# New figures in a list scheduler's tables, and the grouped attention's steps dealt out over all turns of the loop

## The chip, the cores and the metric

One core of a Trainium2 chip runs the kernel. The time is the device time of one execution in microseconds (us). Engines are named as in the profile: PE is TensorE, DVE VectorE, ACT ScalarE, POOL GpSimd and SP SyncE, which issues every load and store here. PEld is TensorE's weight load, SPq and PEq the sequencers.

## What is computed

Two attention blocks over cached keys and values, each with its own projections; their results stand side by side in the output. Block A has 32 query heads over 4 key heads (grouped), block B 32 over 32. All inputs are bf16.

```python
B, Sq, D = 16, 32, 1024;  Hq, Dh, Sk = 32, 128, 1024      # Hkv: 4 in A, 32 in B
q = (x @ wq).reshape(B, Sq, Hq, Dh).transpose(0, 2, 1, 3)
k, v = jnp.repeat(k_cache, Hq // Hkv, axis=1), jnp.repeat(v_cache, Hq // Hkv, axis=1)
p = softmax(einsum("bhqd,bhkd->bhqk", q, k) * Dh ** -0.5)
o = einsum("bhqk,bhkd->bhqd", p, v)
block = o.transpose(0, 2, 1, 3).reshape(B, Sq, Hq * Dh) @ wo
out = jnp.concatenate([block_A, block_B], axis=-1)
```

## The kernel before

`build` lists the work as operations, each with its engine, what it reads and writes, and a duration; `list_schedule` then puts them in the order in which each engine runs them. The 512 tokens are four groups G of 128.

**Block B** runs in 128 steps, one for each turn of the loop. A step (a quad) takes two batches by two heads. Its keys are one load of 1 MB into `KB_sb` (2 slots, L813), its values two loads of 0.5 MB into `VB_sb` (3 slots, L828). VectorE transposes the keys in 32x32 blocks into `KBt_sb` (two instructions, L848); a key slot is free when both are done. TensorE makes the scores as 32 matmuls on 32x32 tiles in `ps_s` (L887, entered as four operations of 8), ScalarE takes the exponential with the row sum (L907), TensorE transposes P (L921) into `ps_pt`, ScalarE copies that to `PT_sb`, TensorE multiplies with the values into `ps_o` (L971, 32 matmuls), VectorE normalizes into `OB_sb` (L987), and TensorE (L992, the OT transpose) and ScalarE turn the result into `OTB_sb`. Four quads share one `G` and one block of four heads.

**Block A** also has 128 steps, two for each key head and batch: `KA_sb` and `VA_sb` loads of 256 KB (L808, L820), key transposes on TensorE (L839) with a copy, scores (L865), exponential (L901), product with the values (L937, in `ps_kt`; GpSimd has copied them to `VAp_sb`, L822), normalizing (L947, L949) and a transpose (L955). A's steps are handed to the scheduler between B's: after turn t, as many as keep A at `t * NIT / NAS`, where `NIT` is 128 and `NAS = int(NIT * A_STEPS_FRAC)` is 117.

**Projections.** Queries come from `wq_sb` (four pieces of 256 KB each for A and B, L639), for A by heads (L657), for B by groups (L674); B's queries are also shuffled by TensorE into `QR` (L694). Output projections (L735) add into `acc` on VectorE (L748, L751 the last). All of these, the shuffles too, use one PSUM bank, `ps_pj`: each group must be copied out before the next may start. B's projections for the next block of heads are spread over the turns, and so are A's heads.

**What sets the order.** `list_schedule` keeps a clock for each engine and takes, of the operations that could start next within `look` microseconds of the earliest, the one with the longest remaining path. The durations of `DUR` (or the `dur=` at the operation), `lat` between engines, `DMA_BW` for a load's time, `DMA_MARGIN` (added to the time at which a load may be issued) and `MODE_SWITCH` (added on TensorE between kinds of tiles, `PE_MODE`) enter there, and nowhere in the program that results: engines then run in that order, each waiting on semaphores. SyncE too takes its loads strictly in the order that came out, and a load that waits for its buffer holds those behind it.

Before the loop stand the transposes of x, the first projections of B and the first heads of A.

Of the kernel before, what the change touches and what calls it, by code (L numbers as in the profile page):

```python
# [16 lines left out]
LAZY_PER_STEP = 100  # L17
LAZY_DELAY = 0
QSH_IN_PJ = True
A_STEPS_FRAC = 0.92  # L20
DMA_BW = 330.7e3
SP_STRICT = False
SP_AHEAD = 1.5
DMA_MARGIN = {"kb_dma": 0.5, "vb_dma": 0.5, "ka_dma": 0.5, "va_dma": 0.5}
DMA_MARGIN_DEFAULT = 2.0
PRIO_BONUS = {}
PE_MODE = {"scoresB": 2, "Qshuf": 2, "PVB": 1}
MODE_SWITCH = 0.11

DUR = {  # L30
    "scoresB": 1.1, "scoresA": 0.45, "PT_trB": 0.50, "PVB": 0.8, "OT_tr": 0.10, "KTA_tr": 0.50,
    "Qshuf": 0.25, "qprojA": 1.8, "qprojB": 1.8, "oprojA": 1.8, "oprojB": 0.9, "xT_tr": 0.5,
    "exp": 1.25, "expA": 1.05, "VAp_cp": 1.2, "normA@dve": 0.42, "OT_trA": 0.2, "OT_evA@dve": 0.35, "PT_ev@act": 0.52, "norm@act": 0.46, "OT_ev@act": 0.24, "KTA_ev@act": 0.93, "qA_ev@act": 0.52, "qB_ev@act": 0.52,
    "QR_ev@act": 0.31, "acc0": 0.52, "xT_ev@act": 0.93, "o_fin@act": 0.52,
    "KBt_tr": 1.15, "recip": 0.15, "norm@dve": 0.30, "PT_ev@dve": 0.62, "OT_ev@dve": 0.16, "KTA_ev@dve": 0.62,
    "QBt_tr": 0.35, "acc+": 0.62, "accF": 0.62, "qA_ev@dve": 0.62, "qB_ev@dve": 0.62, "xT_ev@dve": 0.62, "o_fin@dve": 0.62,
    "QR_ev@dve": 0.35,
    "c0": 0.2, "c1": 0.3,
}


# [20 lines left out]
class Prog:  # L62
# [102 lines left out]
                clk[("eng", op.eng)] = op.sig  # L165
            op.clock = clk

    def simulate(self, lat=0.12, dma_bw=DMA_BW, dma_lat=1.8, jitter=0.0, seed=0):
        rstate = [seed * 2654435761 % 2147483647 + 1]

        def uni(a_, b_):
            rstate[0] = (rstate[0] * 48271) % 2147483647
            return a_ + (b_ - a_) * (rstate[0] / 2147483647.0)
        free = {}
        dma_free = 0.0
        pe_mode = 0
        for op in self.ops:
            ready = 0.0
            for d in op.deps:
                if d.dma_key is None and d.eng == op.eng and op.eng == "pe":  # L180
                    continue
                if d.t1 + lat > ready:
                    ready = d.t1 + lat
            st = max(ready, free.get(op.eng, 0.0))
            jf = 1.0 + (uni(-jitter, jitter) if jitter else 0.0)
            if op.eng == "pe":
                m = PE_MODE.get(op.name, 0)
                if m != pe_mode:
# [12 lines left out]
        return max(op.t1 for op in self.ops)

    def list_schedule(self, lat=0.12, dma_bw=DMA_BW, dma_lat=1.8, look=0.35):
        ops = self.ops
        n = len(ops)
        users = [[] for _ in range(n)]
# [278 lines left out]
def build(nc, pa, pb, out):  # L485
# [13 lines left out]
    HS = 8  # L499
# [21 lines left out]
    with contextlib.ExitStack() as stack:  # L521
# [123 lines left out]
        def qprojA_head(s_, hh):  # L645
            h = s_ * HS + hh
            lazy_flush(("wq", 0, h // MS))
            hc = h % MS
            for t0 in range(0, NTOK, 512):
                tn = min(512, NTOK - t0)  # L650

                JS = 2 if DJ % 2 == 0 else 1
                for j0 in range(0, DJ, JS):
                    def e_qp(e, t0=t0, tn=tn, j0=j0):
                        last = None
                        for j in range(j0, j0 + JS):
                            last = e.matmul(ps_pj[:, 0:tn], wq_sb[:, 0, j, hc * Dh:(hc + 1) * Dh], xT_sb[:, 0, j, t0:t0 + tn],  # L657
                                            start=(j == 0), stop=(j == DJ - 1))
                        return last
                    pcs = sorted(set(j * WQP // DJ for j in range(j0, j0 + JS)))  # L660
                    pr.add("pe", e_qp, reads=[("wq", 0, k_) for k_ in pcs] + [("xT", 0, t) for t in range(NG)], writes=[BK_PJ], name="qprojA",
                           dur=0.225 * JS, rtag=dict((("wq", 0, k_), h // MS) for k_ in pcs))
                evac(QT_sb[:, s_ % 2, t0 // Sq:(t0 + tn) // Sq, hh, :], ps_pj[:, 0:tn].rearrange("p (b q) -> p b q", q=Sq),
                     reads=[BK_PJ], writes=[BK_PJ, ("QT", s_ % 2, hh)], name="qA_ev", wtag={("QT", s_ % 2, hh): s_})

        def qprojB(m_, G):
            lazy_flush(("wq", 1, m_))

# [53 lines left out]
        def oproj(pi, blk, G):  # L722
# [7 lines left out]
            for oh in range(NOH):  # L730
                for h0_ in range(0, nh, 2):
                    def e_op(e, oh=oh, h0_=h0_):
                        last = None
                        for hh in range(h0_, h0_ + 2):
                            last = e.matmul(ps_pj[:, 0:OUTW], OT[:, gp, hh, :], wo_[:, hh, oh * OUTW:(oh + 1) * OUTW],  # L735
                                            start=(hh == 0), stop=(hh == nh - 1))
                        return last
                    pr.add("pe", e_op, reads=[("OT", pi, gp, h0_), ("OT", pi, gp, h0_ + 1), (wo_res, h0_), (wo_res, h0_ + 1)], writes=[BK_PJ],
                           name="oprojA" if pi == 0 else "oprojB",
                           dur=0.45 * OUTW / 512, rtag={(wo_res, h0_): blk, (wo_res, h0_ + 1): blk, ("OTv", pi, gp): (blk, G)})  # L740
                a_ap = acc[:, pi, G, oh * OUTW:(oh + 1) * OUTW]
                o_ap = ost[:, oh * OUTW:(oh + 1) * OUTW]
                if nblk == 1:
# [109 lines left out]
        def st_scores(q):  # L853
# [3 lines left out]
            if q.pi == 0:  # L857
# [73 lines left out]
        def st_pvA(q):  # L931
# [32 lines left out]
        def st_pv(q):  # L964
# [228 lines left out]
```

## Time and profile before

| | |
|---|---|
| median of 3 runs (lowest, highest) | 917.7 us (912.47, 920.21) |
| profiled execution, its time | 913.31 us |
| its span in the trace | 911.5 us |
| mean granted clock of TensorE | 0.962 |
| busy: PE, DVE, ACT | 783.4, 519.3, 462.1 us |
| moved by SyncE's queue | 339.78 MB |

The span runs from the first to the last instruction. A view by windows gives each engine's busy time in a stretch, the number of its instructions, the granted clock as a share of full speed (PEclk), and the mean busy share and rate of the 16 DMA engines. Matmuls overlap, so what one costs is read from the starts of neighbouring groups.

### The profile page before, as it was taken

The page shows a single profiled execution, that of the slowest core. Times are in us where ns is not written, and L with a number is a line of the kernel's source. Part 1 is how long each engine was busy: PE and PEld are TensorE (multiplying, and loading weights), DVE is VectorE, ACT ScalarE, POOL GpSimd, SP SyncE. Part 2 cuts the span into 40 slices and gives each one's busy share as a digit, 9 for nine tenths or more (in the row PEclk, how much of TensorE's full clock was granted, in tenths as well). Part 3 has the DMA queues.
Part 4 walks back from the last instruction along what each step waited for, and adds up shares of the span by engine and source line. Part 5 has one row for each costly group of instructions (what it writes and reads, how often), then busy time and mean ns, then how long its engine had stood idle before and what let it go on. Part 6 is the DMA issues. An engine that isn't in the chain of part 4 may idle for free.

```text
span 911.5 us, 28186 instructions
## 1 busy us (share of the span) xinstructions
PE 783.4 (86%) x12610; PEld 432.9 (47%) x12610; DVE 519.3 (57%) x891; ACT 462.1 (51%) x853; POOL 67.9 (7%) x76
## 2 busy tenths in 40 slices
PE   5879999999998899988898789989897888978775
PEld 2325564545554454545454455536453445545332
DVE  1415655466645566555756556666665656666553
ACT  2215665655564455655564555555554544646242
POOL 0000000100110010101010010001010100001000
PEclk7879999999999999999999999999999899989898
DMA  9789899999999999999999999999999999899995
GB/s 333 270 302 370 308 399 361 402 385 390 359 380 409 411 349 400 401 381 392 368 405 403 411 374 390 375 346 397 405 408 399 385 398 403 333 409 397 385 410 190
DMA packets 151934, 341.64 MB, mean 375 GB/s; under 512 B 10496, under 2 KB 26880, under 8 KB 151808
## 3 DMA queue, kind: packets, MB, share of 16 engines
q1 hardware_dynamic: 151808, 339.78, 97.6%
q8 instruction: 101, 1.65, 0.7%
q14 instruction: 25, 0.20, 0.1%
HBM read 337.64 MB, written 2.10 MB: 373 GB/s over the span
## 4 chain that ended last, share of the span: by engine, by line
PE 56%; ACT 14%; DVE 13%; DMA 12%; issue 2%; SPq 2%; POOL 0%; POOLq 0%; DVEq 0%; ACTq 0%
PE ps_pj L735 10%; PE ps_s L887 10%; DVE KBt_sb L848 6%; PE ps_o L971 6%; PE ps_pj L657 6%; PE ps_pt L921 6%; ACT P_sb L907 5%; PE ps_pj L674 5%; PE ps_kt L937 4%; DMA KB_sb<-in_B_k_cache_dram 4%; ACT PTA_sb L901 3%; PE ps_s L865 3%; DMA wq_sb<-in_A_wq_dram 3%; DVE acc L748 3%; PE ps_kt L839 2%
## 5 line engine op out<-in xcount | busy, mean ns | idle before, releaser
L848 DVE STREAM_TRANSPOSE KBt_sb<-KB_sb 128x1024 f32<-128x1024 f32 x256 | 306.6, 1223 | 46.3 <-DMA KB_sb<-in_B_k_cache_dram 22.6
L887 PE MATMUL ps_s<-KBt_sb,QR 32*32 32x512 bf16 x4096 | 167.0, 402 | 13.8 <-ACT P_sb L907 7.4
L901 ACT ACTIVATE PTA_sb<-ps_s 128x1024 bf16<-128x1024 f32 x128 | 131.6, 1029 | 73.1 <-PE ps_s L865 59.9
L907 ACT ACTIVATE P_sb<-ps_s 128x1024 bf16<-128x1024 f32 x128 | 131.7, 1029 | 70.3 <-PE ps_pt L921 36.5
L588 ACT COPY PT_sb<-ps_pt 128x512 f32<-128x512 f32 x128 | 74.9, 585 | 150.6 <-PE ps_o L971 116.5
L822 POOL COPY VAp_sb<-VA_sb 128x1024 bf16<-128x1024 bf16 x64 | 66.6, 1040 | 770.5 <-DMA VA_sb<-in_A_v_cache_dram 667.3
L921 PE MATMUL ps_pt<-id,P_sb 128*128 128x128 f32 x512 | 91.7, 302 | 18.4 <-ACT P_sb L907 16.9
L987 DVE TENSOR_SCALAR OB_sb<-ps_o,rinv_all 128x128 bf16<-128x128 f32 x128 | 44.4, 347 | 108.0 <-PE ps_o L971 107.6
L921 PEld LDWEIGHTS ps_pt<-id,P_sb 128*128 128x128 f32 x512 | 74.2, 208 | 43.2 <-ACT P_sb L907 25.2
L971 PE MATMUL ps_o<-VB_sb,PT_sb 128*32 128x128 bf16 x4096 | 84.9, 224 | 8.4 <-DMA VB_sb<-in_B_v_cache_dram 6.7
L865 PE MATMUL ps_s<-QT_sb,KTA_sb 128*128 128x256 bf16 x512 | 85.3, 275 | 4.2 <-ACT PTA_sb L901 2.2
L735 PE MATMUL ps_pj<-woB_sb,OTB_sb 128*128 128x512 bf16 x256 | 75.4, 391 | 12.9 <-DVE acc L748 5.4
L937 PE MATMUL ps_kt<-VAp_sb,PTA_sb 128*128 128x129 bf16 x1024 | 80.3, 221 | 5.4 <-ACT KTA_sb L588 2.3
L971 PEld LDWEIGHTS ps_o<-VB_sb,PT_sb 128*32 128x32 bf16 x4096 | 60.1, 98 | 52.1 <-issue 38.7
L657 PE MATMUL ps_pj<-xT_sb,wq_sb 128*128 128x512 bf16 x256 | 74.0, 406 | 11.4 <-DMA wq_sb<-in_A_wq_dram 4.2
L887 PEld LDWEIGHTS ps_s<-KBt_sb,QR 32*32 32x32 bf16 x4096 | 49.7, 90 | 67.5 <-issue 19.5
L937 PEld LDWEIGHTS ps_kt<-VAp_sb,PTA_sb 128*128 128x128 bf16 x1024 | 64.9, 98 | 31.2 <-issue 13.4
L674 PE MATMUL ps_pj<-wq_sb,xT_sb 128*128 128x512 bf16 x256 | 71.0, 391 | 4.3 <-ACT QR L588 1.8
L735 PE MATMUL ps_pj<-woA_sb,OTA_sb 128*128 128x512 bf16 x256 | 66.9, 389 | 7.4 <-DVE ost L751 4.7
L588 ACT CAST QR<-ps_pj 128x256 bf16<-128x256 f32 x128 | 48.5, 379 | 46.0 <-PE ps_pj L694 43.3
L748 DVE TENSOR_TENSOR acc<-acc,ps_pj 128x512 f32<-128x512 f32 x64 | 43.5, 680 | 44.6 <-PE ps_pj L735 44.2
L865 PEld LDWEIGHTS ps_s<-QT_sb,KTA_sb 128*128 128x128 bf16 x512 | 44.3, 98 | 32.3 <-ACT PTA_sb L901 5.8
(52 smaller groups left out, 574.0 us busy)
## 6 DMA issues: line engine op xcount, KB each, us to landing
KB_sb<-in_B_k_cache_dram SPq DMA_DIRECT2D x128, 1024.0 KB, 8.2
VB_sb<-in_B_v_cache_dram SPq DMA_DIRECT2D x256, 512.0 KB, 8.9
KA_sb<-in_A_k_cache_dram SPq DMA_DIRECT2D x64, 256.0 KB, 9.5
VA_sb<-in_A_v_cache_dram SPq DMA_DIRECT2D x64, 256.0 KB, 7.7
wq_sb<-in_B_wq_dram SPq DMA_DIRECT2D x32, 256.0 KB, 6.9
wq_sb<-in_A_wq_dram SPq DMA_DIRECT2D x32, 256.0 KB, 8.7
woB_sb<-in_B_wo_dram SPq DMA_DIRECT2D x32, 256.0 KB, 8.4
woA_sb<-in_A_wo_dram SPq DMA_DIRECT2D x32, 256.0 KB, 7.8
```

The source lines that it names most:

```text
L588: pr.add("act", lambda e: e.copy(dst_ap, src_ap), reads=reads, writes=writes, name=name + "@act", wtag=wtag, rtag=rtag)
L657: last = e.matmul(ps_pj[:, 0:tn], wq_sb[:, 0, j, hc * Dh:(hc + 1) * Dh], xT_sb[:, 0, j, t0:t0 + tn], start=(j == 0), stop=(j == DJ - 1))
L674: last = e.matmul(ps_pj[:, 0:CW], xT_sb[:, 1, j, G * P:(G + 1) * P], wq_sb[:, 1, j, :], start=(j == 0), stop=(j == DJ - 1))
L735: last = e.matmul(ps_pj[:, 0:OUTW], OT[:, gp, hh, :], wo_[:, hh, oh * OUTW:(oh + 1) * OUTW], start=(hh == 0), stop=(hh == nh - 1))
L848: pr.add("dve", lambda e: e.transpose(KBt_sb[:, sl, t_, :].bitcast(F32), KB_sb[:, rs, t_, :].bitcast(F32)), reads=[("KB", rs)], writes=[(" ...
L865: last = e.matmul(ps_s[:, sbf, c2, i * 2 * P:(i + 1) * 2 * P], KTA_sb[:, sl, c * P:(c + 1) * P], qt, start=True, stop=True)
L887: last = e.matmul(ps_s[32 * cg:32 * cg + 32, sbf, g2, :].rearrange("p (s j) -> p s j", s=16), lhsT, rhs, start=(fp == 0), stop=(fp == 3), ...
L901: pr.add("act", lambda e: e.activation(dst, src, ACTF.Exp, scale=scale), writes=BK_S[sbf] + [("PTA", q.half)], name="expA", rtag={("Sv", s ...
L907: pr.add("act", lambda e: e.activation(dst, src, ACTF.Exp, scale=scale, accum_out=stat[:, 0:1]), writes=BK_S[sbf] + ["P", "rowsum"], name= ...
L921: last = e.transpose(ps_pt32[:, m * P:(m + 1) * P], p32[:, m:Sk // 2:NPK], id32[:])
L937: last = e.matmul(ps_kt[:, qh * OA0:qh * OA0 + Dh + 1], PTA_sb[:, h, c, qh * P:(qh + 1) * P], VAp_sb[:, sl, 4 * h + c, 0:Dh + 1], start=(h ...
L971: last = e.matmul(ps_o[32 * a:32 * a + 32, 0:Dh], PT_pairs[:, c // 2, 32 * a:32 * a + 32, c % 2], VB_sb[:, kvs, a // 2, a % 2, c, :], star ...
```

## The change

New figures in the scheduler's tables: durations of operations, the latency between engines, the DMA rate and margins, and `look`. `A_STEPS_FRAC` becomes 1.0, so `NAS` is 128 and A's steps are dealt out evenly over all turns. No operation is added or removed; two lines fewer stand in the file, so that L887 is L885 afterwards, L971 is L969, and so on.

```diff
-A_STEPS_FRAC = 0.92
-DMA_BW = 330.7e3
+A_STEPS_FRAC = 1.0
+DMA_BW = 390e3
...
-DMA_MARGIN = {"kb_dma": 0.5, "vb_dma": 0.5, "ka_dma": 0.5, "va_dma": 0.5}
-DMA_MARGIN_DEFAULT = 2.0
+DMA_MARGIN = {}
+DMA_MARGIN_DEFAULT = 1.0
...
 DUR = {
-    "scoresB": 1.1, "scoresA": 0.45, "PT_trB": 0.50, "PVB": 0.8, "OT_tr": 0.10, "KTA_tr": 0.50,
...
+    "scoresB": 0.222, "scoresA": 0.222, "PT_trB": 0.235, "PVA": 0.312, "PVB": 0.116, "OT_tr": 0.08, "OT_trA": 0.16,
...
-    def list_schedule(self, lat=0.12, dma_bw=DMA_BW, dma_lat=1.8, look=0.35):
+    def list_schedule(self, lat=0.2, dma_bw=DMA_BW, dma_lat=1.8, look=0.1):
...
-                           writes=BK_S[sbf], name="scoresB", dur=0.275, tag="B%d" % q.t,
+                           writes=BK_S[sbf], name="scoresB", dur=0.222, tag="B%d" % q.t,
...
-                       dur=0.2, tag="B%d" % q.t, rtag={"PT": q.qid, ("VB", kvs, 0): q.kid, ("VB", kvs, 1): q.kid}, wtag={"Ops": q.qid})
+                       dur=0.116, tag="B%d" % q.t, rtag={"PT": q.qid, ("VB", kvs, 0): q.kid, ("VB", kvs, 1): q.kid}, wtag={"Ops": q.qid})
```

What it moves, at three places. The first is SyncE's queue near the start, from the second pieces of wq on. Before:

```order
L639 DMA wq_sb<-in_B_wq_dram 128x2x512 x3
L639 DMA wq_sb<-in_A_wq_dram 128x2x512 x4
L639 DMA wq_sb<-in_B_wq_dram 128x2x512
L828 DMA VB_sb<-in_B_v_cache_dram 128x2x1024 x2
L808 DMA KA_sb<-in_A_k_cache_dram 128x1024
L820 DMA VA_sb<-in_A_v_cache_dram 128x1024
L813 DMA KB_sb<-in_B_k_cache_dram 128x2x2048
L718 DMA woB_sb<-in_B_wo_dram 128x1024 x4
L708 DMA woA_sb<-in_A_wo_dram 128x1024
L639 DMA wq_sb<-in_A_wq_dram 128x2x512 x4
L708 DMA woA_sb<-in_A_wo_dram 128x1024 x5
L813 DMA KB_sb<-in_B_k_cache_dram 128x2x2048
```

Now, from B's output weights on, which stood behind those pieces:

```order
L716 DMA woB_sb<-in_B_wo_dram 128x1024 x4
L811 DMA KB_sb<-in_B_k_cache_dram 128x2x2048
L637 DMA wq_sb<-in_B_wq_dram 128x2x512 x4
L637 DMA wq_sb<-in_A_wq_dram 128x2x512 x4
L806 DMA KA_sb<-in_A_k_cache_dram 128x1024
L818 DMA VA_sb<-in_A_v_cache_dram 128x1024
L811 DMA KB_sb<-in_B_k_cache_dram 128x2x2048 x2
L826 DMA VB_sb<-in_B_v_cache_dram 128x2x1024 x4
L811 DMA KB_sb<-in_B_k_cache_dram 128x2x2048
L637 DMA wq_sb<-in_A_wq_dram 128x2x512 x4
L706 DMA woA_sb<-in_A_wo_dram 128x1024 x8
```

The fifth key load of B stands ahead of all second wq pieces, and four key loads stand ahead of the third wq pieces of A (the last x4 row), where one stood.

The second is TensorE at the same time, about where A's first heads run (`ps_pj<-xT_sb,wq_sb` is a head's projection, x8 for one head). Before:

```order
L992 MATMUL ps_o<-ident,OB_sb 128x128
L657 MATMUL ps_pj<-xT_sb,wq_sb 128x512 x32
L865 MATMUL ps_s<-QT_sb,KTA_sb 128x256 x4
L694 MATMUL ps_pj<-QBt,ident 32x256 x4
L865 MATMUL ps_s<-QT_sb,KTA_sb 128x256 x4
L674 MATMUL ps_pj<-wq_sb,xT_sb 128x512 x2
L887 MATMUL ps_s<-KBt_sb,QR 32x512 x32
```

Now, some rows earlier in the program:

```order
L885 MATMUL ps_s<-KBt_sb,QR 32x512 x32
L655 MATMUL ps_pj<-xT_sb,wq_sb 128x512 x8
L919 MATMUL ps_pt<-id32,P_sb 128x128 x4
L969 MATMUL ps_o<-VB_sb,PT_sb 32x128 x32
L672 MATMUL ps_pj<-wq_sb,xT_sb 128x512 x8
L990 MATMUL ps_o<-ident,OB_sb 128x128
L885 MATMUL ps_s<-KBt_sb,QR 32x512 x32
L969 MATMUL ps_o<-VB_sb,PT_sb 32x128 x32
L655 MATMUL ps_pj<-xT_sb,wq_sb 128x512 x8
```

B's second quad was scored behind A's heads 4 to 7 and A's first steps; now all four quads of B's first group stand between the heads.

The third is TensorE in the loop, around the 45th quad of B (in the trace of before these rows run from 353 to 359 us). Before:

```order
L887 MATMUL ps_s<-KBt_sb,QR 32x512 x24
L694 MATMUL ps_pj<-QBt,ident 32x256 x4
L887 MATMUL ps_s<-KBt_sb,QR 32x512 x8
L921 MATMUL ps_pt<-id32,P_sb 128x128 x4
L992 MATMUL ps_o<-ident,OB_sb 128x128
L735 MATMUL ps_pj<-woB_sb,OTB_sb 128x512 x2
L865 MATMUL ps_s<-QT_sb,KTA_sb 128x256 x4
L735 MATMUL ps_pj<-woB_sb,OTB_sb 128x512 x2
L887 MATMUL ps_s<-KBt_sb,QR 32x512 x16
L971 MATMUL ps_o<-VB_sb,PT_sb 32x128 x32
```

Now, at the 46th quad:

```order
L885 MATMUL ps_s<-KBt_sb,QR 32x512 x32
L655 MATMUL ps_pj<-xT_sb,wq_sb 128x512 x8
L953 MATMUL ps_kt<-ident,OA_sb 128x128 x2
L990 MATMUL ps_o<-ident,OB_sb 128x128
L919 MATMUL ps_pt<-id32,P_sb 128x128 x4
L863 MATMUL ps_s<-QT_sb,KTA_sb 128x256 x4
L969 MATMUL ps_o<-VB_sb,PT_sb 32x128 x32
L733 MATMUL ps_pj<-woA_sb,OTA_sb 128x512 x8
L990 MATMUL ps_o<-ident,OB_sb 128x128
```

A quad's scores stand in one row of 32 where they were cut by shuffles and projections. Over the whole fast program the scores of B take 153 rows (220 before), the products with B's values 128 (141) and the shuffles 121 (125).

## Rows read from the trace of the kernel before

**Rows 1.** The page's busy times, shares and instruction counts of each engine.
```profile
PE 783.4 (86%) x12610; PEld 432.9 (47%) x12610; DVE 519.3 (57%) x891; ACT 462.1 (51%) x853; POOL 67.9 (7%) x76
```

**Rows 2.** Windows over the span: engines, PEclk, DMA share, GB/s.
```profile
core 0: us, PE busy (x) PEld busy (x) DVE busy (x) ACT busy (x) POOL busy (x), PEclk, DMA share, GB/s
0.00:75.00 75.00, 53.77 (x425) 24.32 (x425) 21.69 (x30) 20.47 (x32) 4.37 (x14) 0.82 0.85 303
75.00:100.00 25.00, 23.55 (x391) 13.32 (x378) 13.19 (x26) 14.31 (x27) 2.08 (x2) 1.00 0.87 324
100.00:850.00 750.00, 666.62 (x11067) 375.99 (x11052) 455.25 (x782) 405.63 (x744) 61.38 (x59) 0.98 1.01 388
850.00:911.50 61.50, 39.43 (x758) 19.28 (x758) 29.15 (x54) 21.73 (x51) 0.10 (x1) 0.88 0.84 324
```

**Rows 3.** Windows: the two best stretches of 25 us.
```profile
300.00:325.00 25.00, 21.92 (x376) 12.19 (x364) 14.53 (x24) 11.79 (x24) 2.08 (x2) 0.93 1.04 410
800.00:825.00 25.00, 20.82 (x365) 11.87 (x366) 14.62 (x25) 12.24 (x26) 2.08 (x2) 0.86 1.04 411
```

**Rows 4.** Windows: two of four milder stretches; first, last and sum of the six lowest.
```profile
250.00:275.00 25.00, 23.04 (x368) 14.03 (x350) 12.81 (x25) 15.48 (x27) 3.12 (x3) 1.00 1.01 377
375.00:400.00 25.00, 22.53 (x327) 12.43 (x324) 17.95 (x27) 13.40 (x24) 2.08 (x2) 1.00 1.02 385
...
225.00:250.00 25.00, 23.76 (x399) 13.67 (x391) 15.83 (x31) 13.46 (x24) 3.12 (x3) 1.00 0.96 361
...
775.00:800.00 25.00, 22.17 (x388) 12.87 (x388) 16.64 (x30) 16.05 (x31) 2.08 (x2) 1.00 0.91 339
sum 150.00, PE 136.98 PEld 77.49 DVE 101.14 ACT 78.80 POOL 14.56; mean PE 22.83 PEld 12.92 DVE 16.86 ACT 13.13 POOL 2.43
```

**Rows 5.** Timeline of TensorE: start, duration, engine, line, operation; two groups with their successors.
```profile
99.14 1.13 PE L887 MATMUL ps_s<-KBt_sb,QR 32*32 32x512 bf16 x32
100.20 0.75 PE L921 MATMUL ps_pt<-id,P_sb 128*128 128x128 f32 x4
...
342.83 0.43 PE L887 MATMUL ps_s<-KBt_sb,QR 32*32 32x512 bf16 x8
343.19 0.28 PE L955 MATMUL ps_kt<-ident,OA_sb 128*128 128x128 bf16 x2
```

**Rows 6.** Waits: engine, line, awaited: us in total, times, longest.
```profile
PEld ps_pt L921 <- ACT P_sb L907: 25.2, 27, 1.8
PEld ps_o L992 <- DVE OB_sb L987: 21.3, 51, 1.0
PEld ps_pj L694 <- ACT QR L588: 20.1, 29, 1.6
PEld ps_pj L735 <- DVE acc L748: 15.0, 24, 1.3
...
DVE KBt_sb L848 <- DMA KB_sb<-in_B_k_cache_dram: 22.6, 22, 2.3
```

**Rows 7.** Timeline of SyncE at the start, and one row of its waits.
```profile
40.57 2.59 SPq L639 DMA_DIRECT2D wq_sb<-in_B_wq_dram  x3
...
49.01 0.68 SPq L813 DMA_DIRECT2D KB_sb<-in_B_k_cache_dram  x1
...
61.37 1.92 SPq L639 DMA_DIRECT2D wq_sb<-in_A_wq_dram  x4
...
69.64 0.38 SPq L813 DMA_DIRECT2D KB_sb<-in_B_k_cache_dram  x1
...
SPq L639 <- PE ps_pj L657: 10.9, 5, 9.1
```

**Rows 8.** Groups by line: busy us, mean ns, idle before; A's largest and smallest matmul group, B's largest.
```profile
L848 DVE STREAM_TRANSPOSE KBt_sb<-KB_sb 128x1024 f32<-128x1024 f32 x256 | 306.6, 1223 | 46.3 <-DMA KB_sb<-in_B_k_cache_dram 22.6 <-PE ps_s L887 18.9 <-PE ps_o L971 2.4
L887 PE MATMUL ps_s<-KBt_sb,QR 32*32 32x512 bf16 x4096 | 167.0, 402 | 13.8 <-ACT P_sb L907 7.4 <-DVE KBt_sb L848 4.4 <-ACT QR L588 1.2
L865 PE MATMUL ps_s<-QT_sb,KTA_sb 128*128 128x256 bf16 x512 | 85.3, 275 | 4.2 <-ACT PTA_sb L901 2.2 <-ACT QT_sb L588 0.7 <-DVE KTA_sb L590 0.3
L955 PE MATMUL ps_kt<-ident,OA_sb 128*128 128x128 bf16 x128 | 17.8, 221 | 1.3 <-DVE OA_sb L949 1.0
```

More of the change, by code (lines that the diff above doesn't have):

```diff
@@ L30 @@
 DUR = {
-    "scoresB": 1.1, "scoresA": 0.45, "PT_trB": 0.50, "PVB": 0.8, "OT_tr": 0.10, "KTA_tr": 0.50,
[L32 to L38, printed above, removed]
+    "scoresB": 0.222, "scoresA": 0.222, "PT_trB": 0.235, "PVA": 0.312, "PVB": 0.116, "OT_tr": 0.08, "OT_trA": 0.16,
+    "KTA_tr": 0.62, "Qshuf": 0.11, "qprojA": 0.434, "qprojB": 0.434, "oprojA": 0.434, "oprojB": 0.434, "xT_tr": 0.62, "exp": 1.23,
+    "expA": 1.03, "PT_ev@act": 0.587, "OT_ev@act": 0.27, "OT_evA@dve": 0.3, "QR_ev@act": 0.38, "KTA_ev@act": 1.01,
+    "KTA_ev@dve": 0.685, "qA_ev@act": 0.59, "qA_ev@dve": 0.69, "qB_ev@act": 0.59, "qB_ev@dve": 0.69, "acc0": 0.59, "acc+": 0.68,
+    "accF": 0.68, "xT_ev@act": 1.01, "xT_ev@dve": 0.69, "KBt_tr": 1.23, "QBt_tr": 0.435, "recip": 0.15, "norm@dve": 0.347,
+    "normA@dve": 0.4, "VAp_cp": 1.04, "c0": 0.2, "c1": 0.3,
 }
@@ L166, in finalize, with simulate @@
             op.clock = clk
-    def simulate(self, lat=0.12, dma_bw=DMA_BW, dma_lat=1.8, jitter=0.0, seed=0):
+    def simulate(self, lat=0.2, dma_bw=DMA_BW, dma_lat=1.8, jitter=0.0, seed=0):
         rstate = [seed * 2654435761 % 2147483647 + 1]
@@ L661, in qprojA_head @@
                     pr.add("pe", e_qp, reads=[("wq", 0, k_) for k_ in pcs] + [("xT", 0, t) for t in range(NG)], writes=[BK_PJ], name="qprojA",
-                           dur=0.225 * JS, rtag=dict((("wq", 0, k_), h // MS) for k_ in pcs))
+                           dur=0.217 * JS, rtag=dict((("wq", 0, k_), h // MS) for k_ in pcs))
                 evac(QT_sb[:, s_ % 2, t0 // Sq:(t0 + tn) // Sq, hh, :], ps_pj[:, 0:tn].rearrange("p (b q) -> p b q", q=Sq),
@@ L676, in qprojB @@
                 pcs = sorted(set(j * WQP // DJ for j in range(j0, j0 + JS)))
-                pr.add("pe", e_qp, reads=[("wq", 1, k_) for k_ in pcs] + [("xT", 1, G)], writes=[BK_PJ], name="qprojB", dur=0.225 * JS,
+                pr.add("pe", e_qp, reads=[("wq", 1, k_) for k_ in pcs] + [("xT", 1, G)], writes=[BK_PJ], name="qprojB", dur=0.217 * JS,
                        rtag=dict((("wq", 1, k_), m_) for k_ in pcs))
@@ L739, in oproj @@
                            name="oprojA" if pi == 0 else "oprojB",
-                           dur=0.45 * OUTW / 512, rtag={(wo_res, h0_): blk, (wo_res, h0_ + 1): blk, ("OTv", pi, gp): (blk, G)})
+                           dur=0.434 * OUTW / 512, rtag={(wo_res, h0_): blk, (wo_res, h0_ + 1): blk, ("OTv", pi, gp): (blk, G)})
                 a_ap = acc[:, pi, G, oh * OUTW:(oh + 1) * OUTW]
@@ L866, in e_st @@
                         return last
-                    pr.add("pe", e_st, reads=[("QT", q.s % 2, a) for a in range(HS)] + [("KTA", sl)], writes=BK_S[sbf], name="scoresA", dur=0.225,
+                    pr.add("pe", e_st, reads=[("QT", q.s % 2, a) for a in range(HS)] + [("KTA", sl)], writes=BK_S[sbf], name="scoresA", dur=0.222,
                            tag="A%d" % q.t, rtag=dict([(("QT", q.s % 2, a), q.s) for a in range(HS)] + [(("KTA", sl), q.kid)]),
@@ L940, in st_pvA @@
             for c0 in (0, 2):
-                pr.add("pe", lambda e, c0=c0: e_pv(e, c0), reads=[("PTA", h), ("VAp", sl)], writes=[BK_KT], name="PVA", dur=0.32, tag="A%d" % q.t,
+                pr.add("pe", lambda e, c0=c0: e_pv(e, c0), reads=[("PTA", h), ("VAp", sl)], writes=[BK_KT], name="PVA", dur=0.312, tag="A%d" % q.t,
                        rtag={("PTA", h): q.qid, ("VAp", sl): q.kid}, wtag={"OpsA": q.kid})
```

## The prediction

> **What bounds the kernel now.** I read the busy shares first [rows 1]. TensorE, VectorE and ScalarE are all partly idle, TensorE least: it is busy 783.4 us, 86% of the span. Beside it stand the transfers. All 339.78 MB of them are issued by SyncE, and the next view shows when they flow. In the four long stretches [rows 2] the core moved 303 GB/s up to 75 us, 324 up to 100 us, 388 from 100 to 850 us and 324 at the end. The best single stretches reached 410 and 411 GB/s, and TensorE was no fuller there than elsewhere [rows 3]. So about 405 GB/s is what transfers do here when nothing holds them. At 405 the 339.78 MB would take 839 us. The span is 72 us longer; that is where any gain has to come from.
>
> Where is it lost? From 0 to 100 us the kernel moved 0.303 x 75 + 0.324 x 25 = 30.8 MB, which at 405 takes 76 us: 24 us lost. Between 100 and 850 us the loss is (1 - 388/405) x 750 = 31 us, most of it in a few stretches: six of 25 us, one about every 100 us, fell to 339 GB/s at the lowest and 354 in the mean [rows 4]. At 405 those 150 us would be 131: 19 us. In them TensorE is busy 22.83 of 25 us, against 20.82 and 21.92 in the best stretches. The last stretch loses (1 - 324/405) x 61.5 = 12 us. The remaining 5 are the 1.9 MB that the queues moved besides, and rounding.
>
> So the kernel alternates. Where projections crowd TensorE, buffers come free late and transfers thin out; elsewhere transfers are the limit. Two kinds of TensorE time in the crowded stretches can be removed by order alone: breaks and short waits.
>
> **What a break costs.** A B quad's scores are 32 matmuls on 32x32 tiles. In one piece they take 100.20 - 99.14 = 1.06 us to the next group; a piece of 8 takes 343.19 - 342.83 = 0.36 us [rows 5]. That is 0.029 us a matmul, so 8 are worth 0.23, and 0.13 us is paid for each piece, on leaving it. Entering may cost as much again, which these rows don't settle: 0.13 to 0.26 a piece.
>
> **What the waits cost.** TensorE's weight loads stood idle 21.3 us for OB (51 times), 20.1 us for QR and 15.0 us for acc, the last two because every projection and shuffle shares the one bank ps_pj. For the exponential ahead of the P transposes it stood 25.2 us, 27 times [rows 6].
>
> **The change, part by part.**
>
> *The start.* Before, SyncE's queue put the second wq pieces, each waiting for a projection on TensorE, ahead of the fifth B key load. The wq rows issue at 40.57 and 61.37 us, and the key loads behind them at 49.01 and 69.64 us [rows 7]; SyncE waited up to 9.1 us on one such wq buffer. In the new order the first of these key loads is ahead of the wq pieces and three more stand before the wq_A pieces that wait for heads 4 to 7, while TensorE scores all four quads of the first B group among the first heads. I take 350 GB/s for the first 75 us, half the way from 303 to 405: 22.7 MB in 65 us, 10 us saved, and half the deficit of 75 to 100 us, 3 us. Against that, heads 4 to 7 now find their wq_A behind the woB and key loads, which is 2 MB or some 5 us of transfers, with only the tail of a B quad on TensorE to cover it; I charge 3 us. Net **-10** (0 to -24).
>
> *Fewer breaks.* In the order the scores stand in 153 rows instead of 220, PV of B in 128 instead of 141, the shuffles in 121 instead of 125: 84 pieces fewer. At 0.13 to 0.26 us that is 11 to 21 us of TensorE, say 16.
>
> *Fewer and other waits.* I laid the durations of the trace rows over the rows that stand between producer and consumer. Of 128 OT transposes, 60 had under 0.5 us of other TensorE work behind their PV; now 28. Of 287 groups in ps_pj, 105 were followed by the next user too soon for the evacuation; now 52. The other way: 14 P transposes stood within 1.3 us of their scores, now 34. Halving 21.3 and 20.1 + 15.0 us gives 28 us; 20 more short exponentials at 25.2 / 27 = 0.93 us take back 19. Net 9 us, between -28 and +19.
>
> Together 25 us of TensorE over 911 us, 2.7%. It counts only where TensorE is the limit. That is the six stretches, four milder ones at 377 to 385 GB/s [rows 4], and half the rest of the loop at most: 250 us fully and 500 us at a third make 417 us; 2.7% of it is 11. I take **-10** (bounds: all breaks and halved waits everywhere -34; the new exponential waits alone +12).
>
> *A spread out.* NAS goes from 117 to 128, so A's 128 steps no longer stand in the first 117 turns at 1.094 a turn. A's six matmul groups sum to 365.0 us of matmul time, B's and x's eight to 570.5 [rows 8], so A is 39% of TensorE's work, and 8.6% less of it per turn is 3.4% of TensorE in turns 0 to 116. In the ten stretches, 250 us, that is **-8** (0 to -12). At the end it comes back: 11 turns' worth, 8.6% x 39% x 783 = 26 us of TensorE goes into the last stretch, where it was busy 39.4 of 61.5 us [rows 2]. The free 22 us hold most of it: **+3** (0 to +10). Transfers lose nothing in bytes.
>
> *DMA at 390 instead of 330.7, margins 1.0, smaller look.* No instruction changes; all of it acts through the order counted above. The lowest stretch shows 339 [rows 4] and the best 411 [rows 3], so 390 sits beside the loop's own 388. The Trainium skill, "DMA: Bandwidth & Descriptors", section Specifications, lists an HBM limit of about 358 GB/s per core; by it the old 330.7 was the better figure and no reordering could help a kernel that already averages more. The trace doesn't agree: 388 over 750 us [rows 2].
>
> Sum: -10 - 10 - 8 + 3 = -25. The profiled execution took 913.3 us (span 911.5), so 888 on its own scale. It lies under the median of the runs, 917.7, by a factor 1.0048: **892 us**.
>
> **The rivals.**
>
> *A. Only the start gains.* If 388 GB/s is what this mix of loads can do, because wq rows of 1 KB and wo rows are slower than keys, TensorE's relief in the loop is idle time moved elsewhere. For it: transfers count as busy throughout (share 1.01 from 100 to 850 us). Against: rates below 370 only where TensorE is fullest. 913 - 10 + 3 = 906, on the median 910. Chance 0.17; about half of it beyond 1%. By the page's 358 GB/s the result would be this one or no change; the 411 in rows 3 is why I give it no more.
>
> *B. Slower: VectorE held by late keys.* VectorE runs in order, and KBt transposes now stand where a 390 GB/s queue would have delivered. In the weight-heavy stretches the queue gives 354: over six of 25 us it falls (1 - 354/390) x 150 = 14 us behind, and over the first 100 us, at 308, another 21. What stands behind a waiting transpose on VectorE are norm, acc and KTA copies, and TensorE waits for these. Now VectorE waits 22.6 us for keys, 22 times, 1 us each [rows 6]. If the 35 us come on top and the start gains nothing, 913 - 18 + 3 + 35 = 933, median 937. It decides from the point where these waits pass about 50 us in all. Against: the same lag also means later buffers for nobody, and VectorE is busy 519.3 us in all, 306.6 of it with these transposes [rows 1, 8], so there is room to catch up. Chance 0.11.
>
> *C. The loop saturates.* If relief and even spreading let transfers reach 405 almost everywhere, 24 us at the start less 5, and 25 of the loop's 31 go: 913 - 44 = 869, median 873. Chance 0.12.
>
> **How the numbers follow.** Forecast (880 to 904) 0.60, A 0.17, B 0.11, C 0.12. A run within 1% of 917.7 (908.5 to 926.9) counts as no change, about what a measurement of this kernel can tell. Faster: 0.60 + 0.12 + some 0.06 of A = 0.78; the rest of A and a little of B is same, 0.12; slower 0.10. The range must reach C's 873 with a margin and A's 910 with one: 868 to 915, leaving out B and the outer edges.
>
> **What would show it.** Right: the first 75 us above 340 GB/s and no SyncE wait near 9 us at a wq load; the lowest 25 us stretch of the loop above 355; TensorE's idle for OB near 11 us, that for the exponential up by ten or more; TensorE fuller than 39 of the last 61 us. Wrong: VectorE waiting over 50 us for KB_sb (B), loop rate still 388 with TensorE less busy (A), or TensorE saturated and transfers thin after 850 us, which would mean that spreading A cost more than 10 us at the end.

## The result and the profile after

The changed kernel takes 874.8 us (median of 4 runs, 873.4 to 881.4) where the kernel before took 918.7 in the same comparison: a ratio of 0.955, 95% interval 0.948 to 0.961. Ratios here and below are of the means of the fast executions, so they can differ a little from the ratio of two medians. The profiled execution took 873.43 us with a span of 871.6, 39.9 us less than the span before. The prediction was 892 us in a range of 868 to 915; the sign and the range held, and the gain was 1.6 times the 25 us forecast on the span's scale.

The same four stretches of the changed kernel, in windows over the span (engines' busy time with instruction counts, PEclk, DMA share, GB/s; the last one is shorter because the span is):

```profile
0.00:75.00 75.00, 56.32 (x611) 29.85 (x620) 29.40 (x42) 27.44 (x47) 4.32 (x14) 0.98 1.00 376
75.00:100.00 25.00, 24.43 (x373) 16.21 (x380) 12.06 (x25) 15.83 (x27) 4.16 (x4) 1.00 0.91 336
100.00:850.00 750.00, 641.12 (x11324) 389.80 (x11434) 461.70 (x805) 414.56 (x772) 59.30 (x57) 0.98 1.04 403
850.00:871.60 21.60, 10.94 (x195) 5.61 (x182) 8.16 (x21) 4.75 (x11) 0.10 (x1) 0.92 0.41 146
```

Beside [rows 2] they say where the time went. By 100 us 0.376 x 75 + 0.336 x 25 = 36.6 MB have moved instead of 30.8; at 405 GB/s the 5.8 MB are 14 us. From 100 to 850 us it is 302 instead of 291 MB, 28 us. At the end the new kernel loses 13.8 us of transfer time (21.6 us at 146 GB/s) against 12.3 before, so 1.5 us are lost again. The sum is 40.5 us; the spans say 39.9. This is bookkeeping with fixed bytes: it tells where the rate rose, not why.

The thin stretches of the loop are gone. Cut into pieces of 25 us, the loop before had six below 370 GB/s [rows 4]; the lowest of the changed kernel has 380:

```profile
175.00:200.00 25.00, 21.19 (x325) 12.27 (x332) 14.31 (x24) 10.85 (x20) 2.08 (x2) 0.93 0.99 380
```

The start, in SyncE's timeline (start, duration, operation):

```profile
37.99 0.43 SPq L811 DMA_DIRECT2D KB_sb<-in_B_k_cache_dram  x1
41.62 1.92 SPq L637 DMA_DIRECT2D wq_sb<-in_B_wq_dram  x4
44.48 2.05 SPq L637 DMA_DIRECT2D wq_sb<-in_A_wq_dram  x4
...
47.56 1.81 SPq L811 DMA_DIRECT2D KB_sb<-in_B_k_cache_dram  x2
...
57.84 0.37 SPq L811 DMA_DIRECT2D KB_sb<-in_B_k_cache_dram  x1
59.66 1.90 SPq L637 DMA_DIRECT2D wq_sb<-in_A_wq_dram  x4
```

The fifth key load goes out at 37.99 us instead of 49.01 and the sixth at 47.56 instead of 69.64 [rows 7], with the seventh right behind it.

TensorE and VectorE, in the waits and the groups by line, which answer to [rows 6, 8]:

```profile
DVE KBt_sb L846 <- DMA KB_sb<-in_B_k_cache_dram: 63.6, 70, 2.7
...
PEld ps_pt L919 <- ACT P_sb L905: 28.4, 39, 1.4
...
PEld ps_o L990 <- DVE OB_sb L985: 13.2, 27, 0.8
...
PEld ps_pj L692 <- ACT QR L586: 8.0, 14, 1.1
...
PEld ps_pj L733 <- DVE acc L746: 6.2, 14, 0.8
...
L885 PE MATMUL ps_s<-KBt_sb,QR 32*32 32x512 bf16 x4096 | 151.8, 399 | 12.5 <-DVE KBt_sb L846 6.4 <-ACT P_sb L905 2.4 <-issue 1.8
```

The scores of B cost 15.2 us less TensorE time (167.0 before, [rows 8]) for 67 fewer pieces, 0.23 us a piece. The waits for OB, QR and acc fell by 8, 12 and 9 us, the one for the exponential rose by 3. VectorE waits for keys more than before, 63.6 us instead of 22.6. The chain of work that ended last tells what bounds the kernel now; on the page its first line reads:

```profile
DMA 37%; PE 35%; DVE 12%; issue 6%; SPq 5%; ACT 3%; POOL 1%; POOLq 0%; DVEq 0%
```

TensorE was 56% of that chain before and transfers 12%. With 403 GB/s moving for 750 us, where the best 25 us before had 411, transfers are the limit of the loop. (PE's busy total on the page, 732.8 us, isn't compared: the trace of after holds 132 matmul records fewer.)

### The profile page after: what moved, and what is told of

Its sections match the earlier page's. It is cut to its first block, busy times and chain, and to the rows that moved or that the text cites. A ratio compares the mean times of both kernels' runs of the same rounds, so it can differ in the third digit from the quotient of the medians.

```text
span 871.6 us, 28060 instructions
## 1 busy us (share of the span) xinstructions
PE 732.8 (84%) x12478; PEld 441.5 (51%) x12610; DVE 511.3 (59%) x891; ACT 462.6 (53%) x853; POOL 67.9 (8%) x76
## 4 chain that ended last, share of the span: by engine, by line
DMA 37%; PE 35%; DVE 12%; issue 6%; SPq 5%; ACT 3%; POOL 1%; POOLq 0%; DVEq 0%
DMA KB_sb<-in_B_k_cache_dram 24%; DVE KBt_sb L846 8%; DMA VB_sb<-in_B_v_cache_dram 7%; PE ps_s L885 7%; PE ps_pj L733 5%; PE ps_pj L655 4%; DMA VA_sb<-in_A_v_cache_dram 4%; PE ps_o L969 3%; PE ps_pt L919 3%; PE ps_kt L935 3%; PE ps_pj L672 3%; PE ps_s L863 2%; SPq L637 2%; SPq L826 2%; ACT P_sb L905 2%
## 5 line engine op out<-in xcount | busy, mean ns | idle before, releaser
L846 DVE STREAM_TRANSPOSE KBt_sb<-KB_sb 128x1024 f32<-128x1024 f32 x256 | 306.6, 1225 | 71.0 <-DMA KB_sb<-in_B_k_cache_dram 63.6
L885 PE MATMUL ps_s<-KBt_sb,QR 32*32 32x512 bf16 x4096 | 151.8, 399 | 12.5 <-DVE KBt_sb L846 6.4
L919 PE MATMUL ps_pt<-id,P_sb 128*128 128x128 f32 x512 | 88.9, 296 | 16.9 <-ACT P_sb L905 16.5
L969 PE MATMUL ps_o<-VB_sb,PT_sb 128*32 128x128 bf16 x4096 | 81.5, 222 | 21.4 <-DMA VB_sb<-in_B_v_cache_dram 16.3
L863 PE MATMUL ps_s<-QT_sb,KTA_sb 128*128 128x256 bf16 x512 | 82.5, 274 | 8.9 <-ACT PTA_sb L899 6.6
L969 PEld LDWEIGHTS ps_o<-VB_sb,PT_sb 128*32 128x32 bf16 x4096 | 59.7, 97 | 53.4 <-issue 41.8
L885 PEld LDWEIGHTS ps_s<-KBt_sb,QR 32*32 32x32 bf16 x4096 | 56.0, 90 | 59.6 <-DVE KBt_sb L846 11.7
L935 PE MATMUL ps_kt<-VAp_sb,PTA_sb 128*128 128x129 bf16 x1024 | 75.5, 221 | 7.4 <-POOL VAp_sb L820 4.6
L733 PE MATMUL ps_pj<-woB_sb,OTB_sb 128*128 128x512 bf16 x206 | 61.0, 383 | 14.4 <-ACT OTB_sb L586 4.6
L733 PE MATMUL ps_pj<-woA_sb,OTA_sb 128*128 128x512 bf16 x230 | 57.6, 379 | 10.9 <-DMA woA_sb<-in_A_wo_dram 4.0
L655 PE MATMUL ps_pj<-xT_sb,wq_sb 128*128 128x512 bf16 x230 | 61.1, 386 | 6.7 <-DMA wq_sb<-in_A_wq_dram 2.0
L672 PE MATMUL ps_pj<-wq_sb,xT_sb 128*128 128x512 bf16 x226 | 59.2, 392 | 8.5 <-ACT QR L586 3.0
L586 ACT CAST QR<-ps_pj 128x256 bf16<-128x256 f32 x128 | 48.1, 375 | 29.3 <-PE ps_pj L692 27.2
```

The costliest lines, as they stand in the source:

```text
L586: pr.add("act", lambda e: e.copy(dst_ap, src_ap), reads=reads, writes=writes, name=name + "@act", wtag=wtag, rtag=rtag)
L846: pr.add("dve", lambda e: e.transpose(KBt_sb[:, sl, t_, :].bitcast(F32), KB_sb[:, rs, t_, :].bitcast(F32)), reads=[("KB", rs)], writes=[(" ...
L885: last = e.matmul(ps_s[32 * cg:32 * cg + 32, sbf, g2, :].rearrange("p (s j) -> p s j", s=16), lhsT, rhs, start=(fp == 0), stop=(fp == 3), ...
L919: last = e.transpose(ps_pt32[:, m * P:(m + 1) * P], p32[:, m:Sk // 2:NPK], id32[:])
L935: last = e.matmul(ps_kt[:, qh * OA0:qh * OA0 + Dh + 1], PTA_sb[:, h, c, qh * P:(qh + 1) * P], VAp_sb[:, sl, 4 * h + c, 0:Dh + 1], start=(h ...
L969: last = e.matmul(ps_o[32 * a:32 * a + 32, 0:Dh], PT_pairs[:, c // 2, 32 * a:32 * a + 32, c % 2], VB_sb[:, kvs, a // 2, a % 2, c, :], star ...
```

## The experiments

Every run is compared with the kernel before on the same chip. The rates of its profile from 0 to 100 and from 100 to 850 us place its gain: the kernel before has 308 and 388 GB/s, the changed one 366 and 403.

| run | what is new | ratio to before (95%) | GB/s to 100 us | 100 to 850 us |
|---|---|---|---|---|
| changed kernel | all | 0.955 (0.948 to 0.961) | 366 | 403 |
| e1 | latency and look | 0.988 (0.983 to 0.993) | 343 | 390 |
| e2 | DMA rate and margins | 0.993 (0.989 to 0.996) | 315 | 390 |
| e3 | A's spread | 1.002 (0.999 to 1.005) | 324 | 385 |
| e4 | durations | 1.056 (1.048 to 1.064) | 310 | 366 |
| e5 | all but DMA rate and margins | 1.004 (1.001 to 1.008) | 323 | 380 |
| e6 | all but durations | 0.959 (0.953 to 0.965) | 370 | 402 |
| e7 | all but latency and look | 0.963 (0.956 to 0.970) | 341 | 399 |
| e8 | all but A's spread | 0.954 (0.948 to 0.960) | 330 | 404 |
| e9 | order of loads alone | 1.053 (1.042 to 1.063) | 278 | 373 |
| e10 | order of compute alone | 1.179 (1.165 to 1.194) | 336 | 330 |
| e11 | all but the margins | 0.959 (0.951 to 0.967) | 363 | 400 |
| e12 | all, rate 405 | 0.953 (0.946 to 0.959) | 359 | 403 |

### One part of the change alone

**Latency and look (e1).**

```diff
-    def list_schedule(self, lat=0.12, dma_bw=DMA_BW, dma_lat=1.8, look=0.35):
+    def list_schedule(self, lat=0.2, dma_bw=DMA_BW, dma_lat=1.8, look=0.1):
```

> The kernel before with two figures changed alone: latency 0.12 to 0.2 and look 0.35 to 0.1. Its order has 151 rows of B's scores (220 before, 153 after the whole change), but the durations, the DMA rate and the spread of A are the old ones. If breaks on TensorE are what thinned the transfers out, this alone brings most of the loop's gain: 885 to 895 us, 100 to 850 us at 398 GB/s or more. If the DMA figures do it (SyncE's order), it stays at 905 to 918 and 388 GB/s.

Measured: 909.3 us, ratio 0.988. By line, B's scores; in windows, the loop:

```profile
L887 PE MATMUL ps_s<-KBt_sb,QR 32*32 32x512 bf16 x4096 | 154.9, 408 | 17.5 <-DVE KBt_sb L848 13.5 <-ACT P_sb L907 1.2 <-DVE rinv_all L979 0.6
...
100.00:850.00 750.00, 656.41 (x11110) 384.61 (x11116) 451.25 (x786) 404.84 (x746) 61.49 (x59) 0.98 1.02 390
```

The breaks are gone (151 rows of scores) and TensorE saves 12.1 us on that line, yet the loop moves 390 GB/s against 388. Most of what the profiled execution gains (8.9 us of span) lies before 100 us: 343 GB/s against 308 is 3.5 MB, 9 us. Removing breaks didn't fill the transfers.

**DMA rate and margins (e2).**

```diff
-DMA_BW = 330.7e3
+DMA_BW = 390e3
...
-DMA_MARGIN = {"kb_dma": 0.5, "vb_dma": 0.5, "ka_dma": 0.5, "va_dma": 0.5}
-DMA_MARGIN_DEFAULT = 2.0
+DMA_MARGIN = {}
+DMA_MARGIN_DEFAULT = 1.0
```

> The kernel before with DMA_BW 390 and the new margins alone. Its order has 205 rows of B's scores, nearly as many as before. If the order of the loads is the cause, most of the 44 us come here: 880 to 890 us. If breaks and waits on TensorE are, only the start gains: 900 to 912 us, with 388 to 392 GB/s from 100 to 850 us.

Measured: 909.3 us, ratio 0.993, 390 GB/s in the loop. As the breaks' theory had it, in time and rate; but e1 had just taken that theory's own gain away, so neither cause alone was enough.

**A's spread (e3).**

```diff
-A_STEPS_FRAC = 0.92
+A_STEPS_FRAC = 1.0
```

> The kernel before with A_STEPS_FRAC 1.0 alone, 226 rows of B's scores. The prediction's term was -8 in the loop and +3 at the end: 908 to 915 us, TensorE busier than 39 us in the last 61. If even spreading is the main cause, below 895.

Measured: 918.1 us, ratio 1.002. No gain at all, and the loop at 385. TensorE did get fuller at the end, as expected (48.1 of the last 63.4 us), so A's work moved; the transfers didn't follow.

**Durations (e4).** `DUR` and the `dur=` at the operations as in the changed kernel, all else as before.

```diff
-    "scoresB": 1.1, "scoresA": 0.45, "PT_trB": 0.50, "PVB": 0.8, "OT_tr": 0.10, "KTA_tr": 0.50,
+    "scoresB": 0.222, "scoresA": 0.222, "PT_trB": 0.235, "PVA": 0.312, "PVB": 0.116, "OT_tr": 0.08, "OT_trA": 0.16,
...
```

> The kernel before with the new durations alone, 213 rows of B's scores. If breaks count, little changes in the loop: 900 to 915 us. If the durations' effect on which wait is covered counts by itself, below 895, with TensorE's idle for OB and QR halved as after the whole change (13.2 and 8.0 us).

Measured: 964.0 us, ratio 1.056. Both theories missed: the new figures alone make the kernel 48 us slower. The windows of its loop and its waits:

```profile
100.00:850.00 750.00, 641.73 (x10402) 356.93 (x10405) 428.13 (x736) 382.93 (x704) 57.21 (x55) 0.98 0.96 366
...
DVE KBt_sb L846 <- DMA KB_sb<-in_B_k_cache_dram: 6.6, 9, 2.1
```

VectorE hardly waits for keys (6.6 us), and the loop moves 366 GB/s: the loads are ahead of the compute here, and held back by it. From this came a second theory, balance: the figures don't count by themselves but against each other, since they decide which loads stand beside which compute.

### All but one part

**The old DMA figures back (e5)**, the diff of e2 reversed on the changed kernel.

> The changed kernel with DMA_BW 330.7 and the old margins back. Two theories. Balance (new, from the durations alone being 48 us slower): the figures count only against each other; short durations beside a slow DMA figure make the scheduler take transfers for the only limit, and TensorE's order then leaves it short waits: 920 us or more, under 375 GB/s from 100 to 850 us. Breaks (the prediction's): its 147 rows of B's scores make it as good as the changed kernel but for the start, 875 to 890 us.

Measured: 920.9 us, ratio 1.004. Without the DMA figures nothing of the gain is left, with 147 rows of scores. The time is what balance expected; the loop's rate, 380, is above the 375 that it named.

```profile
100.00:850.00 750.00, 618.45 (x10617) 372.77 (x10718) 438.00 (x754) 395.96 (x728) 57.22 (x55) 0.97 1.00 380
...
SPq L811 <- DVE KBt_sb L846: 280.1, 66, 9.6
```

In the changed kernel the same wait is

```profile
SPq L811 <- DVE KBt_sb L846: 126.4, 43, 6.4
```

So in e5 the loads stand ready and the transposes that free the slots come late. This wait alone doesn't mark a slow kernel, though: e7 below has 200.1 us of it and is fast.

**The old durations back (e6)**, the diff of e4 reversed.

> The changed kernel with the old durations back, 161 rows of B's scores. Balance: long durations beside the fast DMA figure are off the other way, as in the run with DMA alone, with VectorE waiting some 80 us for keys: 895 to 910. Breaks: 880 to 890.

Measured: 879.1 us, ratio 0.959. Balance missed here: most of the gain stays, at 402 GB/s, and the time lies just below the range that the breaks' theory gave. Once the rate, latency and look are right, the exactness of the durations is worth some 4 us at most, and the intervals of the two ratios overlap. And:

```profile
DVE KBt_sb L848 <- DMA KB_sb<-in_B_k_cache_dram: 127.2, 81, 4.9
```

127.2 us of VectorE's waiting for keys stand in a kernel that is 37 us faster than before.

**The old latency and look back (e7)**, the diff of e1 reversed.

> The changed kernel with latency 0.12 and look 0.35 back, 219 rows of B's scores (153). Breaks: most of the loop's gain goes, 895 to 910 us, 390 GB/s or less from 100 to 850. Balance: it keeps most, 878 to 890.

Measured: 884.1 us, ratio 0.963. With 219 rows of scores, all breaks back, the loop still reaches 399 GB/s:

```profile
100.00:850.00 750.00, 651.68 (x11130) 377.63 (x11243) 462.98 (x793) 407.74 (x759) 59.30 (x57) 0.98 1.03 399
```

This is what balance expected; the breaks' theory wanted 390 or less. No 25 us of its loop are below 380 GB/s either; e1, with the breaks gone, has three such stretches below 370. In its profiled execution, the slowest of four, the span is 13.8 us longer than the changed kernel's (9 in the medians), and that lies in both stretches: 341 GB/s against 366 before 100 us are 2.5 MB, about 6 us, and 4 GB/s over the loop 3 MB, about 7.

**The old spread of A back (e8)**, the diff of e3 reversed.

> The changed kernel with A_STEPS_FRAC 0.92 back. The prediction's term was -8 in the loop and +3 at the end, so 878 to 884 us; if A's spread does nothing by itself (as it did alone on the kernel before), 872 to 877.

Measured: 875.3 us, ratio 0.954. No difference from the changed kernel that can be told: A's spread does nothing for the total, alone or beside the rest.

**The old margins back, the rate left at 390 (e11).**

```diff
-DMA_MARGIN = {}
-DMA_MARGIN_DEFAULT = 1.0
+DMA_MARGIN = {"kb_dma": 0.5, "vb_dma": 0.5, "ka_dma": 0.5, "va_dma": 0.5}
+DMA_MARGIN_DEFAULT = 2.0
```

> The changed kernel with the old margins (0.5 for keys and values, 2.0 for weights and x) and the rate left at 390. If the rate is what counts in the DMA figures: 872 to 882 us. If the margins do (weights' loads 1 us earlier, keys' and values' 0.5 us later in the plan): 900 or more, like the run with both old (920.9).

Measured: 876.8 us, ratio 0.959. So within the DMA figures it is the rate: e5 and e11 differ by the rate alone, and lie at 920.9 and 876.8 us. Their first 100 us and e11's loop, e5 first:

```profile
0.00:100.00 100.00, 79.33 (x871) 42.10 (x882) 38.47 (x61) 38.35 (x65) 5.36 (x15) 0.85 0.90 323
0.00:100.00 100.00, 80.00 (x922) 43.96 (x923) 40.38 (x63) 41.71 (x71) 7.44 (x17) 0.98 0.98 363
100.00:850.00 750.00, 655.64 (x11455) 389.38 (x11452) 458.70 (x802) 412.00 (x772) 60.34 (x58) 0.99 1.03 400
```

### Loads in one order, compute in the other

Two runs cross the plans. Both orders are made from the same list of operations (A's spread at 0.92, which e8 showed to be neutral), and each engine keeps its rows of one plan:

```diff
+        for eng in ("pe", "act", "dve", "pool", "sp"):
+            old = not NEW_COMPUTE if eng != "sp" else NEW_COMPUTE
+            chain[eng] = [i for i in seqs[old] if self.ops[i].eng == eng]
```

**New loads, old compute (e9).**

> TensorE, VectorE, ScalarE and GpSimd run the kernel before's order row for row, SyncE issues its loads in the order of the changed kernel with A's spread left at 0.92 (875.3 us). If the order of the loads carries the gain: 875 to 890 us, 398 GB/s or more from 100 to 850 us. If the order of the compute does: 900 to 917. If only both orders from one plan fit: 905 or slower.

Measured: 962.3 us, ratio 1.053. In windows, in SyncE's waits for value slots and in VectorE's for keys (engine, line, awaited: us, times, longest):

```profile
100.00:850.00 750.00, 642.75 (x10557) 360.34 (x10559) 430.50 (x741) 389.46 (x713) 59.30 (x57) 0.97 0.98 373
...
SPq L864 <- PE ps_o L1007: 86.9, 31, 11.2
...
DVE KBt_sb L884 <- DMA KB_sb<-in_B_k_cache_dram: 89.6, 40, 7.4
```

The first of these waits is 40.5 us in the changed kernel and 15.3 before.

**New compute, old loads (e10).** Two of SyncE's 648 loads had to be pulled forward, since the two orders would else wait for each other.

> The other half: the four compute engines run the changed kernel's order (A's spread at 0.92), SyncE issues its loads in the kernel before's order, but for two loads pulled forward because the two orders would else wait for each other. If the order of the compute carries the gain: 875 to 890 us. If the order of the loads does, or the fit: 905 or slower.

Measured: 1078.9 us, ratio 1.179.

```profile
100.00:850.00 750.00, 586.28 (x9476) 349.47 (x9474) 374.82 (x663) 352.74 (x640) 52.01 (x50) 0.92 0.88 330
...
PEld ps_kt L881 <- DMA KA_sb<-in_A_k_cache_dram: 115.2, 28, 12.7
```

TensorE stands 115.2 us for A's key loads, up to 12.7 us at once; in the changed kernel that wait is 7.2 us in all:

```profile
PEld ps_kt L837 <- DMA KA_sb<-in_A_k_cache_dram: 7.2, 13, 1.2
```

Neither order carries the gain by itself. SyncE takes its loads strictly in order, so a load that is planned late for the compute that now comes early holds TensorE (e10), and a load that is planned early waits for its slot while those behind it are missed; that is how the two waits of e9 are read here. The two orders must come from one plan.

### The rate in the plan nearer to the real one

**405 (e12).**

```diff
-DMA_BW = 390e3
+DMA_BW = 405e3
```

> The changed kernel with DMA_BW 405 in place of 390, about the rate that its loop really reaches (403 GB/s from 100 to 850 us). If the plan fits the better, the nearer its rate is to the real one: 866 to 873 us. If 390 is already near enough, since the transfers are now the limit: 872 to 880. If the plan must stay a little slower than the transfers, so that loads come early rather than late: 885 or more, with VectorE waiting over 100 us for keys (63.6 at 390).

Measured: 874.9 us, ratio 0.953. Nothing more is to be had: the loop is at 403 GB/s as before. VectorE waits 83.5 us for keys instead of 63.6 without any loss:

```profile
100.00:850.00 750.00, 660.00 (x11502) 397.70 (x11499) 459.30 (x807) 415.95 (x773) 60.46 (x58) 0.98 1.03 403
...
DVE KBt_sb L846 <- DMA KB_sb<-in_B_k_cache_dram: 83.5, 79, 3.5
```

This run, e8 and e11 are as fast as the changed kernel; none was faster.

## Why the prediction was right, and where it was mis-sized

**What bounds the kernel** held. 405 GB/s as the rate of undisturbed transfers, and the 72 us above that, was the right frame: 40 of them came back. That the time fell into the range is in part luck: of the forecast's four terms only the start had both its reason and about its size, the term that mattered most was missing, and the lower bound had been drawn for rival C.

**The signs.** Most signs of being right came: 376 GB/s in the first 75 us, no wait over 3.2 us at a wq load, no stretch of the loop below 380 GB/s, and TensorE busy 43.1 of the last 61.5 us; its idle time for OB, 13.2 us, is near the 11 named. The exponential's rise by ten or more didn't come. And one sign of being wrong came too, VectorE waiting over 50 us for keys, in a kernel that is faster: it was no sign.

**The start** was forecast at -10 and brought -14. The key loads went ahead of the wq pieces as the orders showed, and the first 75 us ran at 376 GB/s, more than the 350 taken; the second part, 75 to 100 us, gave 336 against the 364 assumed. The rate in the plan has a part in it (e5 323 to 100 us, e11 363), but it can't be pinned on one figure: e2, with the rate but without durations, latency and look, has 315, e1 343, e6 370, e7 341, e8 330. TensorE's granted clock in the first 75 us was 0.82 before and 0.98 in the changed kernel, which might have been a cause. It isn't enough for one: e3 has the higher clock and a slow start, e6 a low clock and the fastest:

```profile
0.00:75.00 75.00, 57.69 (x545) 27.77 (x545) 26.33 (x38) 24.57 (x41) 4.37 (x14) 1.00 0.86 314
0.00:75.00 75.00, 56.06 (x603) 28.71 (x612) 28.18 (x41) 26.41 (x45) 4.32 (x14) 0.86 1.00 379
```

**Breaks and waits**, -10, had the right price and the wrong effect. A piece cost 0.23 us (0.18 in e1), inside the 0.13 to 0.26. The waits for OB, QR and acc fell by 29 us together, against 28 counted, and the exponentials cost 3 us more, not 19. (The bounds given for this term, -34 and +12, don't follow from its parts: all breaks and halved waits are 21 + 28 = 49 us, and the exponentials' 19 less at least 11 of breaks are +8 at most.) But e1 removed the breaks without raising the loop's rate by more than 2 GB/s, and e7 put them back and kept 399. So less or more TensorE time of this kind didn't move the transfers, and the step that failed is "Where projections crowd TensorE, buffers come free late and transfers thin out", with relief of TensorE as the cure. It was full and the transfers thin there at the same time; that made them look like cause and effect.

**A spread out**, -8 and +3, was wrong: e3 and e8 show neither a gain nor a cost in the time.

**"All of it acts through the order counted above"** is the step that should have carried the weight. The DMA rate was given no term of its own. Undone with its margins it costs 46 us (e5, 920.9 against 874.8), and by itself 44 (e5 against e11), as much as the whole measured gain. Behind the start, what was counted in the orders were properties of TensorE's row alone; e9 and e10 show that neither SyncE's row nor the others' gives the gain alone. So the loop's -28 in place of -18 is put down to how the rows fit together. That is argued from what is left: no run shows which rows must stand beside which.

**Rival B** didn't come, and its sign was wrong. It set 50 us of VectorE's waiting for keys as the point where the kernel turns slower. The changed kernel has 63.6, e12 83.5 and e6 127.2, all of them 37 to 44 us faster than before. When transfers are the limit, the engine that takes what they bring waits for them. e5, with 25.3 us of it, and e4, with 6.6, are slow, but so is e9 with 89.6: the size of this wait tells neither way. **Rival A** (388 GB/s is what this mix can do) fell with the loop at 403. **Rival C** gave the number that came: 873 us forecast, 874.8 measured, at a chance of 0.12. The loop did saturate, as it said; but the reason it gave, relief of TensorE and A's even spreading, is what e1, e3, e7 and e8 speak against, and its 19 and 25 us for start and loop were 14 and 28. That it came within 2 us is luck in part.

By the Trainium skill, "DMA: Bandwidth & Descriptors", section Specifications, a core's HBM limit is about 358 GB/s, a stack's 716 divided by two cores. One core runs here, and the trace of after disagrees more plainly than that of before: 403 over 750 us.

**What stays open** is why the rate alone (e2) doesn't raise the loop, while the rate with either the new durations (e7) or the new latency and look (e6, both with A's spread) brings most of it. That something beside the rate is needed is shown. The rate with A's spread alone wasn't run, so these two are the likely partners and not the proven ones; and which order of which rows does it is open.

A caution belongs to all of these runs: any figure reshuffles the whole order, and each setting is one order. The changed kernel has three close neighbours (e8, e11, e12) at 875 to 877 us, so its time isn't the luck of one order. e4 and e5 have no such neighbours.

## What to carry to other kernels

Where one plan orders loads and compute, its transfer rate is a figure to set early, from the rates in a trace, and to test together with the others: here each new figure alone was within 1.2% of before or 5.6% slower, together they gave 4.5%, and 390 and 405 did equally well for a real 403. An order is judged as a whole; better counts on one engine's row say little about a queue that another engine serves in strict order. And when transfers become the limit, waiting for them on the compute engines can grow without being a fault; the rate of the transfers says which it is.

## What was not expected of the hardware

Moving one engine's rows against the others' costs far more than any single wait in the trace before would suggest: 962 us with the new loads beside the old compute, 1079 the other way, with TensorE standing for one load for up to 12.7 us. In that last run the mean granted clock of TensorE is also lower, 0.884 against 0.962 before, and over its last 225 us, of which TensorE was busy 142, it is 0.78, a mean between the two levels of 1.2 and 2.4 GHz:

```profile
850.00:1075.00 225.00, 141.84 (x2258) 79.37 (x2258) 95.95 (x166) 73.06 (x147) 8.42 (x9) 0.78 0.72 268
```

What the lower clock adds to its time isn't separated from the waits. And 403 GB/s held over 750 us with loads of 256 KB to 1 MB in changing order, within 2% of the best 25 us stretch.
